# An adaLN transformer block on one core: LayerNorm roots and a memset moved to GpSimd, GpSimd passes tied to VectorE passes, and masked queries built by one copy and eight transfers

## Chip, core and metric

The kernel runs on one core of a Trainium2 chip. The core has TensorE (PE, matrix products into PSUM), VectorE (DVE), ScalarE (ACT), GpSimd (POOL) and SyncE (SP), whose queue issues most of the transfers. The metric is the device time of one execution in microseconds, as the median of several runs. A profile of one execution shows when each instruction ran.

## What is computed

One adaLN block on 2048 tokens of width 512, bf16, with 32 attention heads of width 16 and an MLP of width 1376. The modulation is six rows made from `c`.

```
mod = silu(c) @ w_mod                      # sa, ca, ga, sb, cb, gb
h   = layernorm(x) * (1 + ca) + sa
qkv = h @ wqkv                             # 32 heads, 16 wide
p   = softmax(q k^T / 4)                   # 32 x 2048 x 2048
x   = x + ga * ((p v) @ wo)
h   = layernorm(x) * (1 + cb) + sb
x   = x + gb * (gelu(h @ w1 + b1) @ w2 + b2)
```

## The kernel before, in words

**Tiling.** Queries are taken in four blocks `b` of 512. In a block, heads are taken four at a time: a *quad* is (block, t) with t from 0 to 7, so there are 32 quads. Each quad meets 16 key tiles of 128, four heads each: an *item* is one head's scores of one key tile, 128 x 512. Scores come from row-tiled matmuls (32 of the 128 rows per head, `qk`, L1024). Heads are 16 wide but a row tile is 32, so two heads share a row tile, and the query operand is kept twice, once with the even heads' rows and once with the odd heads' rows, the other rows zero. That is the masked query tile `qm`, 128 x 2 x 512: `q_proj` (L317) makes the projection, `q_evac` (L326) takes it from PSUM in two DVE passes, each multiplied by a column of `qmask`. A new `qm` is made per (block, ch), with ch = t // 2, 16 in all; `used` says when a buffer of the five is free.

**Exponentials on two engines.** ACT takes 12 key tiles of a quad (15 of the first quad), in units of three items (`pA`) and two items (`pB`) by turns (L1076). DVE takes the key tiles 3, 7, 11, 15: it reads one score row from PSUM, adds a bias and writes int16 (a *pass*, L1142); the int16 read as a 16-bit float is an approximate power of two. Three further copies with an offset are made from and to SBUF (*shifts*, L1163), and the four copies are weighed with scaled values `VV` so that the error averages out. PE multiplies all of them with the values (column-tiled, `do_pv`, L1219) into one PSUM bank `od`. DVE copies `od` to SBUF (`o_sb`, L1258); the row of denominators goes through DRAM to a 128 x 16 layout (`d`, `dall`), DVE inverts it (`rp`, L1269), it goes back as a broadcast (`rb`, four transfers), and GpSimd multiplies (`mult`, L1277).

**Order.** All instructions are placed by a planner written in the kernel: it keeps a clock per engine, guesses of durations (`V_PASS`, `EXP`, `TRIP` and others) and labels with the time at which a result is there. `jobs` are rows of (engine, duration, function) with an earliest point `at`, in quads of progress, and `needs`. Each step function (`pe_step`, `dve_step`, `pool_step`, ...) picks the next thing for a free engine. The engines then run their instructions in that order, each held only by semaphores. Where PE would be idle too long, the planner puts in matmuls with zeros (*fill*, L1240). Around the attention lie jobs for the projections, for LayerNorm (`ln_rows`: `ln_var` and `ln_root` are small DVE instructions, an inverse square root by two Newton steps, L221 to L238, and `ln_norm`, L253), for `W_o_pad` (`load_wo`, L404, a memset and eight transfers; `scale_wo`, L410, eight GpSimd passes), and for the output projection and the MLP of each finished block (`tail_jobs`; its last step multiplies on DVE into `tmp`, L689, and adds on GpSimd, L693). `last_tail` does this for the last block after the attention, by hand.

**Start.** Before the planner's part the kernel loads `x`, makes small constants on DVE, warms PE up, normalises block 0, projects its first key and query chunk. The loads of the other blocks are issued behind a DVE memset of one element (L145) that follows the first statistics.

Of the kernel before, what the change touches and what calls it, by code (L numbers as in the profile page):

```python
# [62 lines left out]
KEEP = (5, 18)  # L63

EARLY = 0.95

# [6 lines left out]
FILL_SHARE = 0.75  # L73
V_PASS = 0.61
V_SHIFT = 0.61
V_EVAC = 0.63
# [17 lines left out]
def adaln_block(ctx: ExitStack, tc: tile.TileContext, A_x, A_wqkv, A_wo, B_x, B_w1, B_b1, B_w2, B_b2,  # L94
# [7 lines left out]
    small = ctx.enter_context(tc.tile_pool(name="small", bufs=2))  # L102
    qmp = ctx.enter_context(tc.tile_pool(name="qmp", bufs=5))

# [5 lines left out]
    W_q = res.tile([P, NC, D], BF16, name="W_q")  # L110
    W_o_pad = res.tile([P, 8, D], BF16, name="W_o_pad")
    ga_b = res.tile([P, D], FP32, name="ga_b")
    gb_b = res.tile([P, D], FP32, name="gb_b")
# [63 lines left out]
    magic = const.tile([P, 12], I32, name="magic")  # L177
    nc.vector.memset(magic, 0x5F3759DF)
    zeros = const.tile([P, 32], BF16, name="zeros")
    nc.vector.memset(zeros, 0.0)  # L180
# [8 lines left out]

    ve_ones(VE, 1.0)  # L190

    sc_bf = const.tile([P, NC], BF16, name="sc_bf")
# [50 lines left out]
    def ln_sqrt(st, n):  # L243
        mv = small.tile([P, 12, 2], FP32, name="mv")
        for t in range(n):
            nc.vector.bn_aggr(out=mv[:, t, :], in_=st[:, t, :])
        rs = small.tile([P, 12], FP32, name="rs")
        nc.scalar.activation(out=rs[:, 0:n], in_=mv[:, 0:n, 1], func=ACT.Sqrt, bias=eps_c)
        nc.vector.reciprocal(out=rs[:, 0:n], in_=rs[:, 0:n])
        return mv, rs  # L250

# [67 lines left out]

    def q_evac(ps, ch, b, both=True):  # L320
        t = qmp.tile([P, 2, 512], BF16, name="qm")
        for par in range(2):
            if par and not both:
                nc.scalar.mul(out=t[:, par, :], in_=ps, mul=qmask[:, par:par + 1])
            else:
                nc.vector.tensor_scalar(out=t[:, par, :], in0=ps, scalar1=qmask[:, par:par + 1], scalar2=None,  # L326
                                        op0=ALU.mult)
        qm[(b, ch)] = t

# [73 lines left out]
    def load_wo(j):  # L403
        nc.vector.memset(W_o_pad, 0.0)  # L404
        for r in range(4):
            for par in range(2):
                nc.sync.dma_start(out=W_o4[32 * r:32 * r + 16, :, par, :], in_=wo_v[r][:, :, par, :])
# [46 lines left out]
    def ln_rows(b, src_of, dst_of, key):  # L454

        rows = []

        def var(j):
            st_of[b] = ln_var(st_of[b], 4)

        def root(j):
            st_of[b] = ln_root(*st_of[b])
        rows += [(DVE_, 1.0, var), (DVE_, 1.2, root)]
        for t in range(4):
            def norm(j, t=t):
                mv, rs = st_of[b]
                ln_norm(src_of(), dst_of(), mv, rs, t, t)
            rows.append((DVE_, 0.36, norm))
        return rows
# [21 lines left out]
    def q_job(at, ch, b, needs=()):  # L491
        proj_job(at, lambda ps, js: q_proj(ps, ch, b, js), lambda ps: q_evac(ps, ch, b), [("h", b), *needs],
                 ("q", ch, b), dur=2 * V_EVAC + 0.1)

# [42 lines left out]

    job(4.5, [(DVE_, 2.2, load_wo)], (), "wo_in")
    for t in range(8):
# [20 lines left out]
    def open_late():  # L560
        pro.close()
        lw = ctx.enter_context(tc.tile_pool(name="latew", bufs=1, side="right"))
        W_1 = lw.tile([P, NC, FPAD], BF16, name="W_1")
        nc.gpsimd.memset(W_1[:, :, F:FPAD], 0.0)
        nc.sync.dma_start(out=W_1[:, :, 0:F], in_=B_w1.rearrange("(j p) n -> p j n", p=P))
        W_2 = lw.tile([P, NFC, D], BF16, name="W_2")
        lr = F - (NFC - 1) * P
        nc.gpsimd.memset(W_2[:, NFC - 1, :], 0.0)
        nc.sync.dma_start(out=W_2[:, 0:NFC - 1, :],
                          in_=B_w2[0:(NFC - 1) * P, :].rearrange("(j p) n -> p j n", p=P))  # L570
        nc.sync.dma_start(out=W_2[0:lr, NFC - 1, :], in_=B_w2[(NFC - 1) * P:F, :])
        b1_bf = lw.tile([P, NFC], BF16, name="b1_bf")
        nc.gpsimd.memset(b1_bf, 0.0)
        nc.sync.dma_start(out=b1_bf[:, 0:NFC - 1], in_=B_b1[0:(NFC - 1) * P].rearrange("(j p) -> p j", p=P))
        nc.sync.dma_start(out=b1_bf[0:lr, NFC - 1:NFC],
                          in_=B_b1[(NFC - 1) * P:F].rearrange("(p o) -> p o", o=1))
        b1c = lw.tile([P, NFC], FP32, name="b1c")
        nc.gpsimd.tensor_copy(out=b1c, in_=b1_bf)
        b2r = lw.tile([1, D], BF16, name="b2r")
        nc.sync.dma_start(out=b2r, in_=B_b2.rearrange("(o f) -> o f", o=1))  # L580
        late.update(W_1=W_1, W_2=W_2, b1c=b1c, b2r=b2r)
        tl = ctx.enter_context(tc.tile_pool(name="tailp", bufs=1, side="right"))
        tl2 = ctx.enter_context(tc.tile_pool(name="tailp2", bufs=2, side="right"))
        late.update(tl=tl, tl2=tl2)

    job(6.5, [(SP_, 0.1, lambda j: open_late())],
        ["mod2", "ga", "gb"] + [("k", 3, b) for b in range(NQB)], "late")
    for b in range(NQB - 1):
        for ch in range(NC):

            idx = 4 * (b + 1) + ch - 5
            q_job(8 * b + 2 * ch + 1.3, ch, b + 1, [("used", idx // 4, idx % 4)] if idx >= 0 else [])
# [4 lines left out]
    def tail_jobs(b):  # L597
# [78 lines left out]
        def down(tt):  # L676
# [10 lines left out]
            def mul(j):  # L687
                j.tmp = late["tl2"].tile([P, D], FP32, name="tmp")
                nc.vector.tensor_tensor(out=j.tmp, in0=j.ps, in1=gb_b, op=ALU.mult)  # L689
# [45 lines left out]
    def last_tail():  # L735

        b = NQB - 1
        tl, tl2 = late["tl"], late["tl2"]
        W_1, W_2, b1c = late["W_1"], late["W_2"], late["b1c"]
# [6 lines left out]
        with tc.tile_pool(name="fps", bufs=5, space=PSUM) as fps:  # L746
# [54 lines left out]
            def down_tile(tt, parts=1):  # L801
                o = tl2.tile([P, D], BF16, name="ob")
                tmp = tl2.tile([P, D], FP32, name="tmp")
                n = D // parts
# [143 lines left out]
    nq = len(quads)  # L948
    dall = const.tile([P, nq, 16], FP32, name="dall")
    clock = 0.0  # L950
    free = [0.0, 0.0, 1.0, 0.0, 0.0]
# [188 lines left out]
    def do_pass():  # L1140
        (qi, kt, r), sd, _, last_row, bank = d_items.popleft()
        nc.vector.tensor_scalar(out=t0[(qi, kt)][:, r, :], in0=sd, scalar1=T_BIAS, scalar2=0.0,  # L1142
                                op0=ALU.add, op1=ALU.max)
        end = run(DVE_, V_PASS)
        bank_rel[bank] = end
# [6 lines left out]
    d_prog = [0.0]  # L1152

    def shift_ready():
        if not shifts:
            return False
# [3 lines left out]
    def do_shift():  # L1160
        qi, kt, j = shifts.popleft()
        t16 = tp.tile([P, 4, 512], I16, name="t16")
        nc.vector.tensor_scalar(out=t16, in0=t0[(qi, kt)], scalar1=float(MJ[j]), scalar2=None, op0=ALU.add)  # L1163
        end = run(DVE_, V_SHIFT)
        t16_seq.append((qi, kt, j))
# [154 lines left out]
    def do_job(o, eng):  # L1320
        if o in jobs:
            jobs.remove(o)
            active.append(o)
            if o.hold >= 0:
                o.bank = next(i for i in range(len(banks)) if seen_by(bank_rel[i]))
                bank_rel[o.bank] = INF
        e, dur, fn = o.rows[o.i]
        fn(o)
        if eng == PE_:
# [74 lines left out]
    def dve_step():  # L1404
# [16 lines left out]
        return False  # L1421

    def pool_step():
        o = job_for(POOL_)
        if o is None:
            return False
        do_job(o, POOL_)
        return True
# [63 lines left out]
```

## Time and profile before

| what | us |
|---|---|
| median of 3 runs | 814.64 (811.18 to 816.45) |
| profiled execution, its own time | 815.01 |
| its span, first to last instruction | 813.1 |
| first exponential starts | 14.98 |
| last exponential of the attention ends | 774.7 |
| ACT busy, DVE busy, PE busy, POOL busy | 756.4, 724.8, 770.4, 70.3 |
| granted TensorE clock, mean | 0.995 |

Times within the span count from its first instruction. A line of the costliest groups reads: source line, engine, operation, output and inputs with their shapes, how often, then busy time and mean duration in ns, then the idle time of the engine in front of these instructions and what ended it. A line of the timeline reads: start, duration, engine, line, operation; in brackets the idle time before it and what released it. A matmul's shown duration, 0.38 to 0.39 us for 512 columns, overlaps the next one's; full-rate matmuls start every 0.215 us.

### The profile page before, as it was taken

Reading aid. Unit: us, or ns where it says so; the run is one execution under the profiler, and the core shown is the slowest. Engines: PE = TensorE matmul, PEld = TensorE weight load, DVE = VectorE, ACT = ScalarE, POOL = GpSimd, SP = SyncE. Lnnn points to the kernel's source line nnn. Section 1 sums busy time; section 2 is a strip of 40 time slices with the busy share of each in tenths; the row PEclk is TensorE's granted clock in tenths of the full one; section 3 lists DMA queues with packets and bytes.
Section 4 is the critical chain, followed back from the end, with each engine's and each line's share of the span. In section 5 each row is a group of like instructions: output and inputs, shape, how many; then the busy total and the mean of one; then the engine's idle time right before and its main releaser. Section 6 shows DMA issues by size and latency. Waiting matters only on the chain.

```text
span 813.1 us, 18148 instructions
## 1 busy us (share of the span) xinstructions
PE 770.4 (95%) x7396; PEld 238.1 (29%) x7462; DVE 724.8 (89%) x1306; ACT 756.4 (93%) x681; POOL 70.3 (9%) x62
## 2 busy tenths in 40 slices
PE   7999999988999999999999999999999999999997
PEld 3422222322222222222222322222222222222254
DVE  8879989999998999998998999988998999889663
ACT  5898999998998999999999999999999999999962
POOL 0000000024000000111100000011100000011100
PEclk9999999999899999999999999999999999999999
DMA  9000001023100000000100000010100000010100
GB/s 307 30 1 16 15 16 33 24 70 87 42 15 16 15 16 2 21 16 28 48 16 16 16 13 5 14 29 22 48 15 16 15 3 15 15 28 23 48 2 29
DMA packets 30426, 24.49 MB, mean 30 GB/s; under 512 B 13473, under 2 KB 24194, under 8 KB 30338
## 3 DMA queue, kind: packets, MB, share of 16 engines
q1 hardware_dynamic: 29650, 22.49, 9.7%
q8 instruction: 60, 0.98, 0.5%
q10 hardware_dynamic: 688, 0.79, 0.3%
q14 instruction: 28, 0.23, 0.1%
HBM read 20.65 MB, written 2.61 MB: 29 GB/s over the span
## 4 chain that ended last, share of the span: by engine, by line
PE 48%; ACT 26%; DVE 15%; issue 10%; DMA 1%; POOL 0%; SPq 0%; ACTq 0%; POOLq 0%; DVEq 0%
PE od L1219 15%; ACT pA L1076 14%; ACT pB L1076 9%; PE sA L1024 7%; PE sB L1024 6%; DVE t L1142 5%; DVE t L1163 5%; PE aux L1024 4%; PE od L1240 3%; PE aux L683 3%; PE aux L620 2%; PE aux L303 1%; PE fb L810 1%; PE aux L658 1%; PE aux L332 1%
## 5 line engine op out<-in xcount | busy, mean ns | idle before, releaser
L1076 ACT ACTIVATE pA<-sA 128x1536 bf16<-128x1536 f32 x310 | 469.7, 1515 | 17.0 <-PE sA L1024 7.1
L1142 DVE TENSOR_SCALAR t<-aux 128x512 int16<-128x512 f32 x500 | 327.9, 679 | 31.9 <-PE aux L1024 30.1
L1076 ACT ACTIVATE pB<-sB 128x1024 bf16<-128x1024 f32 x309 | 337.3, 1091 | 6.3 <-PE od L1219 3.6
L1163 DVE TENSOR_SCALAR t<-t 128x2048 int16<-128x2048 int16 x375 | 260.3, 715 | 2.7 <-PE od L1219 1.6
L1024 PE MATMUL aux<-qm,kT 32*128 32x512 bf16 x500 | 178.2, 382 | 6.5 <-DVE t L1142 3.5
L1024 PEld LDWEIGHTS <-kT 32*128 32x128 bf16 x2048 | 76.7, 91 | 267.6 <-issue 262.9
L1219 PE MATMUL od<-pA,VE 128*32 128x512 bf16 x930 | 142.2, 386 | 0.6 <-DVE o_sb L1258 0.5
L1219 PE MATMUL od<-t,VV 128*32 128x512 f16 x1500 | 140.0, 386 | 2.6 <-DVE t L1163 2.4
L1219 PE MATMUL od<-pB,VE 128*32 128x512 bf16 x618 | 141.3, 386 | 0.1
L1024 PE MATMUL sA<-qm,kT 32*128 32x512 bf16 x930 | 124.1, 385 | 10.2 <-ACT pA L1076 5.0
L1024 PE MATMUL sB<-qm,kT 32*128 32x512 bf16 x618 | 121.3, 385 | 5.4 <-ACT pB L1076 2.2
L1277 POOL TENSOR_TENSOR OT<-o_sb,rb 128x512 bf16<-128x512 f32 x31 | 42.2, 1362 | 559.1 <-DMA rb<-d 360.8
L1219 PEld LDWEIGHTS <-VE 128*32 128x32 bf16 x2048 | 50.5, 95 | 95.1 <-issue 82.3
L1240 PE MATMUL od<-hT,zeros 128*32 128x512 bf16 x836 | 75.5, 386 | 0.0
L1219 PEld LDWEIGHTS <-VV 128*32 128x32 bf16 x1500 | 39.8, 95 | 60.6 <-issue 51.7
L1219 PE MATMUL od<-t,VE 128*32 128x512 f16 x500 | 49.4, 386 | 2.7 <-DVE o_sb L1258 2.7
L683 PE MATMUL aux<-W,uG 128*128 128x512 bf16 x120 | 35.5, 383 | 1.6 <-issue 1.6
L658 PE MATMUL aux<-h2T,W 128*128 128x512 bf16 x113 | 35.6, 385 | 0.4 <-issue 0.3
L1240 PEld LDWEIGHTS <-zeros 128*32 128x32 bf16 x864 | 21.8, 95 | 35.9 <-issue 30.8
L663 DVE TENSOR_SCALAR uG<-aux,b1c 128x512 bf16<-128x512 f32 x33 | 24.3, 737 | 4.7 <-PE aux L658 4.7
L620 PE MATMUL aux<-W_o_pad,OT 128*128 128x512 bf16 x88 | 25.6, 382 | 0.7 <-issue 0.5
L693 POOL TENSOR_TENSOR ob<-tmp,xr 128x512 bf16<-128x512 f32 x12 | 15.6, 1304 | 116.5 <-DVE tmp L689 116.5
(157 smaller groups left out, 428.3 us busy)
## 6 DMA issues: line engine op xcount, KB each, us to landing
rb<-d SPq DMA_DIRECT2D x124, 64.0 KB
W_m<-in_w_mod_dram SPq DMA_DIRECT2D x2, 1024.0 KB
xr<-in_A_x_dram SPq DMA_DIRECT2D x4, 512.0 KB
out_dram<-ob SPq DMA_DIRECT2D x15, 128.0 KB
xb<-in_A_x_dram SPq DMA_DIRECT2D x3, 512.0 KB
W<-in_B_w_dram SPq DMA_DIRECT2D x1, 1376.0 KB
W<-in_B_w_dram SPq DMA_DIRECT2D x1, 1280.0 KB
W_m<-in_w_mod_dram SPq DMA_DIRECT2D x1, 512.0 KB
```

The costliest lines, as they stand in the source:

```text
L620: nc.tensor.matmul(out=j.ps, lhsT=OT[(b, t)][:, tt * P:(tt + 1) * P], rhs=W_o_pad[:, t, :], start=False, stop=(t == 7))
L658: nc.tensor.matmul(out=j.ps, lhsT=late["W_1"][:, c, fc * P:(fc + 1) * P], rhs=T["h2"][:, c, :], start=(c == 0), stop=(c == NC - 1))
L663: nc.vector.tensor_scalar(out=T["u"][:, fc, :], in0=j.ps, scalar1=late["b1c"][:, fc:fc + 1], scalar2=None, op0=ALU.add)
L683: nc.tensor.matmul(out=j.ps, lhsT=T["u"][:, fc, tt * P:(tt + 1) * P], rhs=late["W_2"][:, fc, :], start=False, stop=(fc == NFC - 1))
L693: nc.gpsimd.tensor_tensor(out=o, in0=j.tmp, in1=T["x1"][:, tt, :], op=ALU.add)
L1024: nc.tensor.matmul(out=dst, lhsT=kT[32 * r:32 * r + 32, ch, kt * P:(kt + 1) * P], rhs=qm[(b, ch)][32 * r:32 * r + 32, par, :], start=True, ...
L1076: nc.scalar.activation(out=pt[:, 0:n, :], in_=st[:, 0:n, :], func=ACT.Exp, scale=math.log(2.0) / STEP)
L1142: nc.vector.tensor_scalar(out=t0[(qi, kt)][:, r, :], in0=sd, scalar1=T_BIAS, scalar2=0.0, op0=ALU.add, op1=ALU.max)
L1163: nc.vector.tensor_scalar(out=t16, in0=t0[(qi, kt)], scalar1=float(MJ[j]), scalar2=None, op0=ALU.add)
L1219: nc.tensor.matmul(out=od[qi][32 * r:32 * r + 32, :], lhsT=w, rhs=src, start=first, stop=last_)
L1240: nc.tensor.matmul(out=dst[32 * r:32 * r + 32, :], lhsT=zeros, rhs=hT[:, r, 0:512], start=bank is not None, stop=bank is not None)
L1277: nc.gpsimd.tensor_tensor(out=OT[(b, t)], in0=o, in1=j.rb, op=ALU.mult)
```

## The change

- `ln_rows` calls `ln_mean` (DVE, only the aggregation) and `ln_pow` (GpSimd: add EPS, then a power of -0.5 with a constant tile) in place of `ln_var` and `ln_root`. It is used for blocks 1 to 3 at the start and for the three tails; block 0, the last tail and the general path keep what they had.
- A `qm` is no longer made by two masked passes: one DVE pass scales the projection into a staging tile `q_st` (two buffers), and eight transfers on SP of 16 rows each bring the even and odd heads' rows into one of five fixed buffers. Four of these are cleared by GpSimd at the start; the first query chunk still uses the two masked passes, into the fifth buffer. In the planner a query job has a fourth row on SP of 5.5 us.
- `W_o_pad` is cleared by GpSimd, not DVE.
- The planner starts a GpSimd row of over 1 us, once progress is past 0.95, only when DVE starts something that is not a shift, or after a wait of up to 9 us. It puts a one-element GpSimd copy (`mark`) that reads the output of DVE's previous pass or shift in front of it, and keeps shifts from starting until the row's planned end.
- The product `tmp` of the MLP's last step has one buffer, not two.

```
+Q_BUFS = 5
+Q_TRIP = 5.5
+POOL_WAIT = 3.0
+POW = 0.8
...
+    qm_buf = [res.tile([P, 2, 512], BF16, name=f"qm{i}") for i in range(Q_BUFS)]
...
+    for i in range(1, Q_BUFS):
+        nc.gpsimd.memset(qm_buf[i], 0.0)
...
+    def ln_pow(mv, n):
+        rs = small.tile([P, 12], FP32, name="rs")
+        nc.gpsimd.tensor_scalar(out=rs[:, 0:n], in0=mv[:, 0:n, 1], scalar1=EPS, scalar2=None, op0=ALU.add)
+        nc.gpsimd.tensor_tensor(out=rs[:, 0:n], in0=rs[:, 0:n], in1=mhalf[:, 0:n], op=ALU.pow)
+        return mv, rs
...
+    def q_stage(ps):
+        st = qst.tile([P, 512], BF16, name="q_st")
+        nc.vector.tensor_scalar(out=st, in0=ps, scalar1=Q_SCALE, scalar2=None, op0=ALU.mult)
+        return st
+
+    def q_rows(st, ch, b):
+        t = qm[(b, ch)] = qm_buf[(4 * b + ch) % Q_BUFS]
+        for par in range(2):
+            for r in range(4):
+                rows = slice(32 * r + 16 * par, 32 * r + 16 * par + 16)
+                nc.sync.dma_start(out=t[rows, par, :], in_=st[rows, :])
...
-        nc.vector.memset(W_o_pad, 0.0)
+        nc.gpsimd.memset(W_o_pad, 0.0)
...
-        rows += [(DVE_, 1.0, var), (DVE_, 1.2, root)]
+        rows += [(DVE_, 0.6, var), (POOL_, POW, root)]
...
-        proj_job(at, lambda ps, js: q_proj(ps, ch, b, js), lambda ps: q_evac(ps, ch, b), [("h", b), *needs],
-                 ("q", ch, b), dur=2 * V_EVAC + 0.1)
...
+        job(at, [(PE_, 2 * MM, f(0)), (PE_, 2 * MM, f(1)), (DVE_, V_EVAC, stage),
+                 (SP_, Q_TRIP, lambda j: q_rows(j.st, ch, b))], [("h", b), *needs], ("q", ch, b), 2)
...
-    job(4.5, [(DVE_, 2.2, load_wo)], (), "wo_in")
+    job(4.5, [(POOL_, 3.6, load_wo)], (), "wo_in")
...
-                j.tmp = late["tl2"].tile([P, D], FP32, name="tmp")
+                j.tmp = late["tl1"].tile([P, D], FP32, name="tmp")
...
     def shift_ready():
-        if not shifts:
+        if not shifts or clock < port[0]:
             return False
...
+        if eng == POOL_ and dur > 1.0:
+            if dve_now["prev"] is not None and dve_now["start"] > clock - DT / 2:
+                nc.gpsimd.tensor_copy(out=mark[0:1, 0:1], in_=dve_now["prev"][0:1, 0:1])
+            port[0] = clock + dur
...
     def pool_step():
         o = job_for(POOL_)
         if o is None:
             return False
+        if o.rows[o.i][1] > 1.0 and progress() > EARLY and (d_tiles or d_items or shifts):
+            now = dve_now["start"] > clock - DT / 2 and dve_now["free"] and dve_now["prev"] is not None
+            since = pool_since.setdefault((o.label, o.i), clock)
+            if not (now and (d_items or clock > since + POOL_WAIT)) and clock < since + 3.0 * POOL_WAIT:
+                return False
         do_job(o, POOL_)
         return True
```

## Prediction

> **What bounds the kernel now.** I read the page first: the busy shares, then the costliest groups.
>
> ```profile
> span 813.1 us, 18148 instructions
> PE 770.4 (95%) x7396; PEld 238.1 (29%) x7462; DVE 724.8 (89%) x1306; ACT 756.4 (93%) x681; POOL 70.3 (9%) x62
> ...
> PE 48%; ACT 26%; DVE 15%; issue 10%; DMA 1%; POOL 0%; SPq 0%; ACTq 0%; POOLq 0%; DVEq 0%
> ...
> L1076 ACT ACTIVATE pA<-sA 128x1536 bf16<-128x1536 f32 x310 | 469.7, 1515 | 17.0 <-PE sA L1024 7.1
> L1142 DVE TENSOR_SCALAR t<-aux 128x512 int16<-128x512 f32 x500 | 327.9, 679 | 31.9 <-PE aux L1024 30.1
> L1076 ACT ACTIVATE pB<-sB 128x1024 bf16<-128x1024 f32 x309 | 337.3, 1091 | 6.3 <-PE od L1219 3.6
> L1163 DVE TENSOR_SCALAR t<-t 128x2048 int16<-128x2048 int16 x375 | 260.3, 715 | 2.7 <-PE od L1219 1.6
> ...
> L1277 POOL TENSOR_TENSOR OT<-o_sb,rb 128x512 bf16<-128x512 f32 x31 | 42.2, 1362 | 559.1 <-DMA rb<-d 360.8
> ```
>
> Three engines look full, so the shares do not decide. The table by stretch of time does (us; busy time of PE, PEld, DVE, ACT, POOL; clock, DMA).
>
> ```profile
> 150.00:175.00 25.00, 22.47 (x247) 6.98 (x248) 24.64 (x40) 23.26 (x21) 5.13 (x4) 1.00 0.05 13
> 200.00:225.00 25.00, 22.94 (x233) 5.77 (x232) 23.76 (x38) 21.08 (x19) 2.26 (x2) 0.86 0.12 34
> 225.00:275.00 50.00, 47.38 (x463) 14.64 (x464) 45.88 (x89) 45.66 (x41) 2.66 (x2) 1.00 0.06 13
> 275.00:325.00 50.00, 48.30 (x467) 13.88 (x473) 46.44 (x77) 49.95 (x41) 2.54 (x2) 1.00 0.06 13
> 750.00:775.00 25.00, 24.42 (x255) 7.43 (x255) 14.25 (x25) 24.96 (x23) 2.80 (x2) 1.00 0.14 39
> ```
>
> From 275 on ACT is full (49.95 of 50) while DVE has slack, and from 750 to 775 DVE is done early (14.25 of 25). So ACT's exponentials set the length of the attention part. In the trace they follow each other at best every 1.33 us (three items) and 0.90 us (two): 310 x 1.33 + 309 x 0.90 = 690 us of the 760 us between the first (14.98) and the last one's end (774.7). Casts, three Gelus with their table loads take some 27 us; pauses make up the rest. Pauses over 0.15 us in front of the next ACT instruction, start to start, add up to 33 us. Only they, the 15 us before and the 38 us after can change.
>
> The third view is the order of time where ACT pauses longest.
>
> ```profile
> 196.69 4.30 POOL L410 TENSOR_TENSOR W_o_pad<-W_o_pad,ga_b 128x512 bf16<-128x512 bf16 x3
> 196.97 4.56 DVE L1163 TENSOR_SCALAR t<-t 128x2048 int16<-128x2048 int16 x3
> ...
> 200.02 0.40 PE L1219 MATMUL od<-t,VV 128*32 128x512 f16 x4 [0.58 <-DVE t L1163]
> ...
> 201.59 0.62 PE L1219 MATMUL od<-t,VV 128*32 128x512 f16 x4 [0.95 <-DVE t L1163]
> ...
> 202.85 1.45 ACT L1076 ACTIVATE pA<-sA 128x1536 bf16<-128x1536 f32 x1 [2.03 <-PE sA L1024]
> ```
>
> Three shifts (DVE, int16 from and to SBUF) take 4.56 us instead of 3 x 0.68: each that meets a GpSimd pass ends only after it. PE waits for them, then ACT for PE, and matmuls run at 0.60 us instead of 0.39 until about 209 (clock 0.86). Passes from PSUM beside GpSimd stay at 0.67 to 0.69 us. Of 375 shifts, 18 are stretched over 0.72 us, by 13.0 us in all, the longest to 1.76.
>
> **The change, part by part.** The exponentials (619), passes (500) and shifts (375) keep their numbers in the changed program, so ACT's 690 us stay, and a saving on DVE counts only where ACT waits for it.
>
> *GpSimd tied to passes.* The pauses that stand directly behind stretched shifts are 1.4 + 0.3 us near 171, 2.1 + 1.2 + 0.8 + 0.3 near 200 to 208, and 1.0 at 491: 7.1 us. In the changed program, of 51 tied GpSimd operations nearly all follow a shift and have two passes (or copies from PSUM) behind them before the next shift: 2 x 0.60 us start to start. Mark (0.1 to 0.2, from the small GpSimd rows, 0.10 to 0.19) and operation (1.16 to 1.27) take about 1.4, so a shift still waits some 0.2 us, 51 x 0.2 = 10 us, but in small pieces that DVE's slack covers (by the same table it is idle 39 of the 500 us between 225 and 725). If that cover is gone, up to 3 us of it comes back. I take -6.5; bounds -3 and -11 (a quarter of the remaining small pauses, some 17 us, gone too).
>
> *Masked queries.* Removed: 15 of 30 evacuations at 0.74 us (spacing 0.66), 10 us of DVE: hidden, since DVE is not the bound, 0 (bounds -2, 0). Added: 15 x 8 transfers on SP. The eight W_o_pad transfers of before took SP 3.64 us, 0.455 each; from issue to what waits for it a transfer of this queue took 1.7 to 1.8 us (d at 64.16, dall at 65.99). So a query is ready 0.74 + 0.1 + 7 x 0.455 + 1.8 = 5.8 us after its evacuation starts, against 1.4 before: 4.4 later. Where the projection lies a quad or more ahead (twelve jobs for later blocks) that is nothing. For (0,1) it is not: evacuation at 72.33, first use at 76.84, so it would come 72.33 + 5.8 = 78.2, 1.3 late. The order confirms it: between that projection and that first use PE now has 86 matmuls instead of 58, 32 of them fill instead of 16: 28 x 0.054 (four share 0.215 us) = 1.5, with some six more changes of kind at 0.1 (0.32 from a column group to a row in place of 0.215) 2.1. I take +1.8 (bounds 1.3, 2.6). The other two, (0,2) and (0,3), lie 15 and 16 items ahead of use, 6.7 and 7.2 us at 2.23 us for five items: enough. Behind the first of these jobs on SP stands quad 0's denominator; it is issued up to 3.6 us later, but its reciprocal is ten DVE instructions (some 6.5 us) behind, so 0, bound +2 (DVE would wait with passes behind it).
>
> *Rest of the order.* Counting PE's groups between score matmuls in both programs (0.215 a group, 0.1 a change), stretches longer than ACT's pair of 2.23 us, Gelus apart, sum to 1.3 us more in the changed one beyond quad 2; fill grows from 216 to 249 groups. +1.3 (bounds -1, +2.5).
>
> *Root on GpSimd.* Nine small DVE instructions, 15.42 to 17.21: 1.79 us, six times, 10.7 us of DVE. In their place two GpSimd instructions and two hand-overs. The power has no row; the nearest are 0.19 (cast, 128x11) and 1.27 (tensor-tensor, 128x512): with the add and 0.3 of semaphores 0.7 to 1.8, so the chain gets 0 to 1.1 us shorter. Only block 1's first chain is on the path (ACT pauses 2.48 us at 22.7 for its values). Nearest in size is the small row, halved because a power is not a cast: -0.5 (bounds -1.1, +2).
>
> *Memsets on GpSimd.* W_o_pad: DVE loses 1.77; GpSimd needs, from 0.205 (128 columns) and 0.524 (512), 0.83 ns a column, 3.5 us, in which shifts wait; three passes and a copy stand behind it: 0 (bounds -1, +1). Four query buffers at the start, 0.95 us each from about 1.4 us on, beside DVE's first small operations. The row nearest is the 128x4 `var`, 0.91 us instead of 0.17 beside a GpSimd pass. Two operations there are like it (`qmask`, `ce`): two half memsets, +0.9, and all of it is on the path, since the first load of block 1 is issued behind them. Bounds 0 and +3.6 (every small one waits for a whole memset). By the Trainium skill (SBUF — State Buffer, Who interferes with whom) a copy, cast or tensor_scalar in a two-port mode is fully blocked until the GpSimd instruction ends; the 0.91 us agrees, but no run here shows a GpSimd memset doing it. By that rule the one-column operations could be blocked too, and the sum would go towards the upper bound.
>
> Sum against the profiled execution (815.0, its span 813.1 and 1.9 around it; the median of the runs is 814.6): -6.5 + 1.8 + 1.3 - 0.5 + 0.9 = -3.0, **812.0**. The tail's single `tmp` is written and read on DVE in order: nothing.
>
> **Rivals.**
> - *The tie does not hold* (slower). After the mark the multiplication still waits for `rb`; 18 of 31 started when that transfer landed. If it lands over 0.2 us after the mark, the operation runs into the next shift as before, and the -6.5 goes to 0: 818.5. For it: those 18 waits, and SP now carries 55 us more of issues. Against it: six of the 7.1 us stand behind W_o_pad's scaling, which waits for no transfer.
> - *GpSimd is slow at the start* (slower). What block 1's chain gains is replaced by a longer pause of ACT at 22 us. With a power of 3.35 us, the longest elementwise row of the trace (DVE's reciprocal of 128x512), the chain takes 0.19 + 3.35 + 0.3 = 3.8, 2.0 more than now; with that and the memsets' upper bound the time is 812.0 + 0.5 + 2.0 + 2.7 = 817.2. A power over 1.3 us decides it. Against: the first tensor-tensor on GpSimd (74.5) took 1.267 us, like the others. The Trainium skill (GPSIMD Engine Reference, Instruction dispatch) gives about 6 us for the first call of freshly loaded code; no row here shows it, and by it the sum would be near 818 without the memsets.
> - *More pauses go* (faster). If the small pauses were mostly DVE's lateness too, its 22 us of lighter load take 10 of the 17 us: 802. For: DVE is at 24.6 of 25 in 150 to 175. Against: their releaser is PE, and after 275 DVE has 2 to 6 us of slack per 50.
> - *The change does nothing net*: ties gain what the query wait costs, 815.
>
> **How the numbers follow.** Forecast (808 to 816, with the do-nothing case at its edge) 0.55; tie fails 0.17; slow start 0.13; more pauses go 0.15. Two in ten left out at the outside of the outer cases: range 804 to 821. A measurement of this kernel tells about 1% (8.1 us) from no change. Below 806.9: the third rival and a sliver, 0.17. Above 823.2: 0.13 of the 0.30 of the two slower cases, where the upper bounds of the query wait (+0.8), the denominator (+2), the order (+1.2) and DVE's lost cover (+3) come on top. Within: 0.70.
>
> **What would show it.** ACT's exponentials stay at 619, its pauses near 170 and 200 to 208 go, and a pause of about 2 us stands before the third quad's first scores, with PE waiting for `qm<-q_st`. Shifts: mean from 715 ns to about 700, none near 1.7 us. DVE's busy time falls by 20 us or so, without ACT's falling. The first exponential starts about 0.9 us later than 14.98. Wrong would be: shifts of 1.5 us again (tie fails), a power over 1.3 us, the first exponential at 18, or ACT pauses that sum to far less than 28 us.

## The result, and the profile after

The changed kernel took **824.8 us** (median of 4 runs, 823.1 to 828.4) beside 815.6 us (median of 4 runs) of the kernel before: ratio **1.012**, 95% interval 1.008 to 1.016. Predicted were 812.0, range 804 to 821. The profiled execution took 823.1 us with a span of 821.3, 8.2 more than the 813.1 of before.

The page after, its busy shares and ACT's and DVE's largest groups:

```profile
span 821.3 us, 18771 instructions
PE 788.0 (96%) x7594; PEld 240.3 (29%) x7594; DVE 705.7 (86%) x1237; ACT 757.1 (92%) x681; POOL 90.0 (11%) x130
...
L1120 ACT ACTIVATE pA<-sA 128x1536 bf16<-128x1536 f32 x310 | 468.3, 1511 | 12.8 <-PE od L1272 5.4
L1186 DVE TENSOR_SCALAR t<-aux 128x512 int16<-128x512 f32 x500 | 328.4, 681 | 38.1 <-PE aux L1068 36.4
L1120 ACT ACTIVATE pB<-sB 128x1024 bf16<-128x1024 f32 x309 | 335.9, 1087 | 16.0 <-PE od L1272 6.4
L1215 DVE TENSOR_SCALAR t<-t 128x2048 int16<-128x2048 int16 x375 | 259.9, 714 | 6.7 <-PE od L1272 4.7
```

The counts stayed (619 exponentials, 500 passes, 375 shifts), ACT's busy time too (757.1 after 756.4), and DVE lost 19 us. So the extra time is time in which ACT did not compute: its idle time in front of the two groups of exponentials went from 17.0 + 6.3 to 12.8 + 16.0 us.

The table by stretch shows where (after; to be laid beside that of before):

```profile
150.00:175.00 25.00, 24.50 (x251) 6.99 (x248) 22.32 (x40) 23.95 (x22) 2.73 (x4) 1.00 0.09 23
200.00:225.00 25.00, 24.00 (x254) 6.74 (x253) 23.90 (x41) 21.59 (x21) 3.87 (x6) 0.93 0.14 40
225.00:275.00 50.00, 47.67 (x481) 13.82 (x473) 46.47 (x86) 48.39 (x43) 5.12 (x6) 1.00 0.06 16
275.00:325.00 50.00, 48.85 (x452) 13.29 (x444) 45.79 (x75) 48.63 (x40) 2.89 (x4) 1.00 0.08 21
550.00:560.00 10.00, 9.22 (x64) 1.85 (x63) 8.08 (x15) 7.58 (x7) 0.00 (x0) 0.66 0.02 3
750.00:775.00 25.00, 24.69 (x270) 6.98 (x265) 20.96 (x36) 24.85 (x23) 4.00 (x5) 1.00 0.18 50
```

ACT (fourth busy column) gained in the first three rows (23.95 for 23.26, 21.59 for 21.08, 48.39 for 45.66) and lost where it had been full: 48.63 for 49.95 from 275 on, 7.58 for 9.99 between 550 and 560, where the clock column is 0.66. That last stretch in the kernel before:

```profile
550.00:560.00 10.00, 9.84 (x98) 2.85 (x95) 8.65 (x16) 9.99 (x10) 1.16 (x1) 1.00 0.11 29
```

Two sums account for the span of this kernel and of all those below: the start of the first exponential, and ACT's pauses over 0.15 us, counted as in the prediction. Before: 14.98 and 33.0. After: 17.09 and 39.2, so +2.1 and +6.2, against +8.2 of span.

**The start.** The first instructions on GpSimd and DVE (start, duration, engine, line):

```profile
1.35 3.62 POOL L202 MEMSET qm<- 128x1024 bf16 x4
1.44 0.15 DVE L173 TENSOR_SCALAR par_i<-pidx 128x1 int32<-128x1 int32 x1 [1.44 <-POOL pidx L170]
1.63 0.15 DVE L176 CAST pmask<-par_i 128x1 f32<-128x1 int32 x1
1.81 0.15 DVE L177 TENSOR_SCALAR pmask<-pmask 128x1 f32<-128x1 f32 x1
2.00 2.99 DVE L181 TENSOR_SCALAR qmask<-pmask 128x2 f32<-128x2 f32 x1
4.84 0.17 DVE L192 MEMSET ones_row<- 1x128 bf16 x1
```

`qmask` has two columns and takes 0.17 us in the kernel before. Here it ends with the fourth memset, 2.8 us later, and everything behind it on DVE moves: the warm-up's first matmul from 2.67 to 5.37. By the Trainium skill (SBUF — State Buffer, Who interferes with whom) when DVE is in a two-port mode, the engine that issues first holds the shared ports for one whole instruction; the trace agrees that `qmask` is blocked, but it waited for four GpSimd instructions in a row, not for one, and three one-column operations of DVE were not held at all.

**Block 1's LayerNorm.** The root on GpSimd cost what the bounds of the prediction allowed: 1.04 us for the power, a little less than one of GpSimd's 512-column operations (1.15 to 1.27).

```profile
17.13 0.37 DVE L267 BATCH_NORM_AGGREGATE mv<-st 128x2 f32<-128x6 f32 x4
17.59 0.23 POOL L272 TENSOR_SCALAR rs<-mv 128x4 f32<-128x4 f32 x1 [12.61 <-DVE mv L267]
17.90 1.04 POOL L273 TENSOR_TENSOR rs<-rs,mhalf 128x4 f32<-128x4 f32 x1
...
18.98 1.39 DVE L277 TENSOR_SCALAR xb<-xb,mv,rs 128x512 bf16<-128x512 bf16 x4 [1.48 <-POOL rs L273]
```

**The place where ACT had paused longest.** GpSimd's scaling of `W_o_pad` again, with the mark in front of each operation:

```profile
196.09 0.68 DVE L1186 TENSOR_SCALAR t<-aux 128x512 int16<-128x512 f32 x1
196.17 1.15 POOL L443 TENSOR_TENSOR W_o_pad<-W_o_pad,ga_b 128x512 bf16<-128x512 bf16 x1
...
196.69 3.02 DVE L1215 TENSOR_SCALAR t<-t 128x2048 int16<-128x2048 int16 x2
...
197.28 0.18 POOL L1386 COPY mark<-t 1x1 int16<-1x1 int16 x1
197.41 1.15 POOL L443 TENSOR_TENSOR W_o_pad<-W_o_pad,ga_b 128x512 bf16<-128x512 bf16 x1
...
202.77 1.02 ACT L1120 ACTIVATE pB<-sB 128x1024 bf16<-128x1024 f32 x1 [2.71 <-PE aux L1068]
```

GpSimd ran late here, so the mark at 197.28 found its data long there and held nothing. A shift that began at 196.69 waited for the operation in front of it, then for mark and operation behind it: two shifts took 3.02 us in place of 1.28 (back to back without a GpSimd pass), and ACT stopped for 2.9 and 0.8 us. The pauses near 171 are gone (none over 0.15 us is left before the same exponentials), and 0.25 us is left of the 1.0 near 491. Over the kernel 27 shifts are stretched by 12.0 us (18 by 13.0 before).

**New stops.** The longest, apart from the one before the third quad (2.75 us, at 82), stand where PE is never idle. From 429 to 437 (PE's matmuls and ACT's exponentials):

```profile
429.43 0.40 PE L1272 MATMUL od<-pA,VE 128*32 128x512 bf16 x3
429.44 0.39 PE L1272 MATMUL od<-pB,VE 128*32 128x512 bf16 x1
...
431.15 1.04 PE L663 MATMUL aux<-W_o_pad,OT 128*128 128x512 bf16 x4
...
432.62 1.45 ACT L1120 ACTIVATE pA<-sA 128x1536 bf16<-128x1536 f32 x1
432.99 0.39 PE L1068 MATMUL sB<-qm,kT 32*128 32x512 bf16 x2
...
434.82 1.04 PE L663 MATMUL aux<-W_o_pad,OT 128*128 128x512 bf16 x4
435.78 0.39 PE L1272 MATMUL od<-pB,VE 128*32 128x512 bf16 x1
...
436.27 1.02 ACT L1120 ACTIVATE pB<-sB 128x1024 bf16<-128x1024 f32 x1 [2.20 <-PE od L1272]
```

The scores for the next `pB` are there at about 433.4. ACT starts at 436.27, because all four `pB` buffers are taken: PE reads one item of a `pB` at 429.44, and the next, which frees a buffer, only at 435.78, with the output projection (`W_o_pad`) and scores between. That stop is written into the order of PE's instructions.

### The profile page after: what moved, and what is told of

It is laid out like the page before. It is cut to its first block, busy times and chain, and to the rows that moved or that the text cites. A ratio compares the mean times of both kernels' runs of the same rounds, so it can differ in the third digit from the quotient of the medians.

```text
span 821.3 us, 18771 instructions
## 1 busy us (share of the span) xinstructions
PE 788.0 (96%) x7594; PEld 240.3 (29%) x7594; DVE 705.7 (86%) x1237; ACT 757.1 (92%) x681; POOL 90.0 (11%) x130
## 4 chain that ended last, share of the span: by engine, by line
PE 54%; ACT 19%; DVE 15%; issue 7%; DMA 2%; POOL 2%; SPq 0%; POOLq 0%; DVEq 0%; ACTq 0%
PE od L1272 15%; ACT pA L1120 9%; PE sA L1068 7%; PE sB L1068 6%; ACT pB L1120 6%; DVE t L1186 6%; DVE t L1215 5%; PE aux L1068 4%; PE aux L726 3%; PE od L1293 3%; PE aux L663 3%; PE aux L701 3%; ACT uG L715 2%; PE aux L341 1%; PE aux L327 1%
## 5 line engine op out<-in xcount | busy, mean ns | idle before, releaser
L1120 ACT ACTIVATE pA<-sA 128x1536 bf16<-128x1536 f32 x310 | 468.3, 1511 | 12.8 <-PE od L1272 5.4
L1293 PE MATMUL od<-hT,zeros 128*32 128x512 bf16 x940 | 79.8, 383 | 0.0
L1386 POOL COPY mark<-t 1x1 int16<-1x1 int16 x51 | 9.5, 186 | 615.5 <-DVE t L1215 465.9
L1330 POOL TENSOR_TENSOR OT<-o_sb,rb 128x512 bf16<-128x512 f32 x31 | 39.5, 1276 | 14.8 <-DMA rb<-d 10.8
L701 PE MATMUL aux<-h2T,W 128*128 128x512 bf16 x132 | 39.2, 383 | 0.5 <-DVE t L1186 0.4
L726 PE MATMUL aux<-W,uG 128*128 128x512 bf16 x132 | 38.2, 384 | 0.0
L1293 PEld LDWEIGHTS <-zeros 128*32 128x32 bf16 x996 | 23.7, 95 | 37.8 <-issue 30.6
L663 PE MATMUL aux<-W_o_pad,OT 128*128 128x512 bf16 x96 | 27.5, 382 | 0.0
```

Of the source, the lines that this page charges most:

```text
L663: nc.tensor.matmul(out=j.ps, lhsT=OT[(b, t)][:, tt * P:(tt + 1) * P], rhs=W_o_pad[:, t, :], start=False, stop=(t == 7))
L701: nc.tensor.matmul(out=j.ps, lhsT=late["W_1"][:, c, fc * P:(fc + 1) * P], rhs=T["h2"][:, c, :], start=(c == 0), stop=(c == NC - 1))
L726: nc.tensor.matmul(out=j.ps, lhsT=T["u"][:, fc, tt * P:(tt + 1) * P], rhs=late["W_2"][:, fc, :], start=False, stop=(fc == NFC - 1))
L1120: nc.scalar.activation(out=pt[:, 0:n, :], in_=st[:, 0:n, :], func=ACT.Exp, scale=math.log(2.0) / STEP)
L1293: nc.tensor.matmul(out=dst[32 * r:32 * r + 32, :], lhsT=zeros, rhs=hT[:, r, 0:512], start=bank is not None, stop=bank is not None)
L1330: nc.gpsimd.tensor_tensor(out=OT[(b, t)], in0=o, in1=j.rb, op=ALU.mult)
```

## The experiments

After the result there were two theories. **Parts:** the 9 us are the sum of what the changed operations do on the chip (start, query transfers, tie, root). **Order:** the operations cost little, but any change of them or of their planned durations makes the planner write another order of all 18,000 instructions, and the order of before was a favourable one. Every kernel below computes the whole reference. "Planned anew" means that the planner was left to choose; "held" that its inputs stayed as they were and only what a function emits was changed, so that PE's and ACT's orders are identical to those of the kernel named.

| kernel | plan | first exponential | ACT pauses | span | ratio to before |
|---|---|---|---|---|---|
| before | | 14.98 | 33.0 | 813.1 | 1 |
| after | anew | 17.09 | 39.2 | 821.3 | 1.012 (1.008 to 1.016) |
| e1_start | of after | 14.98 | 41.4 | 820.6 | 1.008 (1.005 to 1.010) |
| e2_mask_dve | of after | 17.47 | 48.1 | 831.4 | 1.023 (1.020 to 1.026) |
| e3_no_mark | of after | 17.73 | 41.1 | 823.7 | 1.016 (1.012 to 1.019) |
| e4_q_undone | anew | 16.92 | 31.1 | 813.7 | 0.997 (0.995 to 0.9995) |
| e5_no_tie | anew | 17.01 | 33.1 | 815.6 | 1.006 (1.003 to 1.008) |
| e10_pow_only | anew | 15.45 | 32.8 | 813.9 | 1.007 (1.002 to 1.012) |
| e9_q_early | anew | 16.22 | 40.4 | 820.6 | 1.007 (1.003 to 1.011) |
| e12_q_early_no_tie | anew | 15.42 | 36.7 | 818.6 | 1.004 (1.002 to 1.006) |
| e8_order_b (guess only) | anew | 16.88 | 36.5 | 818.5 | 1.006 (1.002 to 1.009) |
| l4_order_f (guess only) | anew | 17.51 | 36.8 | 819.4 | 1.009 (1.006 to 1.012) |
| e7_order_a (before, guess only) | anew | 15.40 | 39.2 | 820.4 | 1.009 (1.005 to 1.014) |
| l1_order_c (before, guess only) | anew | 15.55 | 39.4 | 820.3 | 1.006 (1.004 to 1.008) |
| l2_order_d (before, guess only) | anew | 16.70 | 34.8 | 816.9 | 1.005 (1.003 to 1.006) |
| f1_pow_held | of before | 15.21 | 35.5 | 815.5 | 1.001 (0.999 to 1.003) |
| f2_q_held | of before | 17.47 | 29.7 | 812.4 | 0.998 (0.996 to 0.9996) |
| f3_both_held | of before | 15.27 | 32.2 | 812.6 | 1.002 (0.999 to 1.005) |

First exponential, pauses and span are of the profiled execution; the two differences add up to that of the span within 1.4 us in every row. The ratio and its interval compare all comparable runs of a kernel with the runs of before made beside them; it is not the quotient of the medians, which for e4 is 0.999, for f3 0.999 and for e9 1.009. In e10 the profiled execution (815.7 us) was the fastest of four with a median of 820.5. In e4, e9, l2 and f2 the first exponential is late for another reason than in the changed kernel: the granted clock there is 0.58 (e4) and 0.72 between 12 and 18 us, and 1.00 in the changed kernel and in f3, which has the same operations at the start as f2.

**The start alone, order of after (e1_start).** The four query buffers are cleared only when block 0's first `hT` is there.

```
-    for i in range(1, Q_BUFS):
-        nc.gpsimd.memset(qm_buf[i], 0.0)
...
+        nc.gpsimd.tensor_copy(out=gate, in_=hT[0:1, 0, 0:1])
+        for i in range(1, Q_BUFS):
+            nc.gpsimd.memset(qm_buf[i], 0.0)
```

> Only the clearing of the four query buffers is moved behind block 0's first hT (a one-element GpSimd copy waits for it); the planned order of everything else is the same. Theory A (the start is held by qmask waiting 2.8 us for all four memsets): the first exponential starts at about 15.0 instead of 17.09, and the time falls by 2.1 us against the changed kernel, to about 822.7. Rival (the start has slack, the memsets only moved a wait): the first exponential stays near 17 and the time near 824.8.

The first exponential is back at 14.98, and the median fell by 3.2 us (821.6), though the two ratios' intervals overlap. So the memsets at the start cost 2 to 3 us, more than the 0.9 predicted and within the bound of 3.6. Two thirds of the loss remain. The profiled spans differ by only 0.7 us: e1's execution was the slowest of its four and has a clock drop more (at 265), the changed kernel's was its fastest.

**The transfers alone, order of after (e2_mask_dve).** The planner still believes in one pass and eight transfers; emitted are two masked DVE passes.

```
-            j.st = q_stage(j.ps)
+            q_evac(j.ps, ch, b)
...
-                 (SP_, Q_TRIP, lambda j: q_rows(j.st, ch, b))], [("h", b), *needs], ("q", ch, b), 2)
+                 (SP_, Q_TRIP, lambda j: None)], [("h", b), *needs], ("q", ch, b), 2)
```

> The planned order is kept instruction by instruction, but each query is masked by two DVE passes into the same buffer, and the 120 transfers are gone (the planner still counts 5.5 us for them). Theory B1 (the stop of ACT before the third quad, 2.7 us, is built into the order by the planner's 5.5 us, with its 33 more fill groups): the stop stays at 1.5 us or more and the time within 1.5 us of the changed kernel. Theory B2 (the transfers are late, eight issues take 5.0 us instead of 3.6): the stop shrinks under 1 us and the time falls by about 2 us. Either way DVE does 15 more passes of 0.66 us.

The stop before the third quad is 2.76 us without a single transfer, 2.75 with them. It is no wait for a transfer; it lies in the order, where the planner, told 5.5 us for a query's way, put the third quad's scores. The time rose by 9 us: 15 more passes of 0.66 us are 9.9 us, so in this fixed order DVE time that the planner had not counted showed nearly in full (time saved on DVE in the order of before did not show, see f3).

**Parts undone, planned anew (e4_q_undone, e5_no_tie, e10_pow_only).** e4: queries as before, the rest as after. e5: no mark, no holding of GpSimd rows or shifts. e10: the kernel before with the root and `W_o_pad`'s memset on GpSimd only (and the fixed `qm` buffers and the single `tmp`).

```
-        job(at, [(PE_, 2 * MM, f(0)), (PE_, 2 * MM, f(1)), (DVE_, V_EVAC, stage),
-                 (SP_, Q_TRIP, lambda j: q_rows(j.st, ch, b))], [("h", b), *needs], ("q", ch, b), 2)
+        proj_job(at, lambda ps, js: q_proj(ps, ch, b, js), lambda ps: q_evac(ps, ch, b), [("h", b), *needs],
+                 ("q", ch, b), dur=2 * V_EVAC + 0.1)
```

```
-                nc.gpsimd.tensor_copy(out=mark[0:1, 0:1], in_=dve_now["prev"][0:1, 0:1])
-            port[0] = clock + dur
+                pass
+            pass
...
-        if o.rows[o.i][1] > 1.0 and progress() > EARLY and (d_tiles or d_items or shifts):
+        if False:
```

> The masked queries are made by two DVE passes again, without transfers and memsets, and planned so; tie, power and W_o_pad's memset stay. Theory A+B: start 2.1 and the stop before the third quad 2.7 go: 4.8 us less than the changed kernel, 820.0, and 4 to 5 more than the kernel before, for the rest. Rival C (the whole loss is the queries): at most 816. Rival D (the loss is order and tie, DVE's 15 passes were worth something): 822 or more.

> No mark, no hold of GpSimd rows, no hold of shifts; queries, power and memsets as changed. Theory E (the tie still brings something, about 3 us, as the pauses near 171 and 491 went): 827 to 829, with shifts stretched by 13 us or more. Rival F (the tie costs more than it brings, through shifts held back and late GpSimd passes): 821 or less.

> The kernel before with the power on GpSimd, W_o_pad's memset on GpSimd and nothing else (queries by two DVE passes, no tie), planned so. If the losses are the queries' (9.8 us with the tie) and the tie's (6.1 us with the queries) each by itself, this is 824.8 - 9.8 - 6.1 = 809, faster than before by 6. If they are one and the same loss seen twice (the tie only hurts a plan with late queries, or the order was unlucky), it is 815 or more.

By the ratios, taken singly, e4 would give the queries 12 us and e5 the tie 5 us of loss, and e10 alone 6 us more than before to the root and the memset: together over 20, where 9 were lost. e4 and e5 each met the expectation that blames its own part (rivals C and F); e10's median of 820.5 met the one by which both were the same loss seen twice. The parts do not add up, which spoke against Parts and led to the next kernels.

**Only a guess changed (e7_order_a, l1_order_c, l2_order_d; e8_order_b, l4_order_f).** The first three are the kernel before, the other two the changed kernel; no operation is changed, only the order and how many fill matmuls the planner adds.

```
-V_PASS = 0.61
+V_PASS = 0.60
```

(e7; l1: `EXP` 0.905 and 1.33 for 0.92 and 1.34; l2: `V_SHIFT` 0.60 for 0.61; e8: `Q_TRIP` 5.7 for 5.5; l4: `POOL_WAIT` 4.0 for 3.0.)

> The kernel before with the planner's guess for a pass at 0.60 us instead of 0.61: the same instructions, in another order. It measures how far the order alone moves the time. Theory L (an order by itself is worth some us either way, and part of the 9 us is that): 3 us or more from 815.5. Rival (order is worth little): within 2 us of it.

> The changed kernel with the planner's guess for a query's transfers at 5.7 us instead of 5.5: the same instructions in another order. Theory L: 3 us or more from 824.8, most likely below it. Rival: within 2 us of it.

> The kernel before, with the planner's guesses for the exponentials set to the measured 0.905 and 1.33 us instead of 0.92 and 1.34: the same instructions in another order. Theory O (the order of the kernel before is a lucky one among many; another costs some 3 to 8 us): 817 to 824, as the 821.2 of e7_order_a. Rival (e7_order_a was the unlucky one): 813 to 816.

> The kernel before with one planner guess changed (a shift 0.60 instead of 0.61), no instruction changed or added but fills; planned anew. Theory Scatter: between 815 and 822, more likely above than below the kernel before, pauses of ACT 34 to 41 us. Rival (the two other orders of before that cost 6 to 7 us were exceptions): within 2 us of before, pauses 31 to 35 us.

> The changed kernel with one planner guess changed (a GpSimd row's longest wait 4.0 times three instead of 3.0 times three), planned anew; the start and all operations as in the changed kernel. Theory Scatter: between 817 and 826, not bound to the changed kernel's 824.8. Rival (the changed kernel's time comes from its operations): 823 to 827.

A change of 0.01 to 0.015 us in a guess costs the kernel before 0.5 to 0.9%, as much as most versions of the changed kernel lost. The clock does not explain it. The time does go with it: the 80 runs of before beside these experiments average 812.7 us where the granted clock is 0.998 or more (16 runs) and 817.6 where it is 0.990 or less (10 runs). But e7, l1 and l2 ran at 0.995 to 0.996 on average, and before at 0.994. One stop that e7 has and before has not (the same kind as at 432 in the changed kernel):

```profile
501.86 1.11 ACT L1076 ACTIVATE pB<-sB 128x1024 bf16<-128x1024 f32 x1
...
502.39 0.39 PE L1024 MATMUL sA<-qm,kT 32*128 32x512 bf16 x3
...
505.39 0.38 PE L1219 MATMUL od<-pA,VE 128*32 128x512 bf16 x1
...
505.87 1.45 ACT L1076 ACTIVATE pA<-sA 128x1536 bf16<-128x1536 f32 x1 [2.89 <-PE od L1219]
```

Scores at 502.4, the exponential at 505.9: again a `pA` buffer that PE read late.

**The operations in the order of before (f1_pow_held, f2_q_held, f3_both_held).** f1: root and `W_o_pad`'s memset on GpSimd. f2: one scaled copy and eight transfers per query, buffers cleared behind block 0's `hT`. f3: both. The planner's rows stay those of before.

```
         def var():
-            st_of[b] = ln_var(st_of[b], 4)
+            st_of[b] = ln_mean(st_of[b], 4)
...
     def q_evac(ps, ch, b, both=True):
...
+        st = qst.tile([P, 512], BF16, name="q_st")
+        nc.vector.tensor_scalar(out=st, in0=ps, scalar1=Q_SCALE, scalar2=None, op0=ALU.mult)
+        for par in range(2):
+            for r in range(4):
+                rows = slice(32 * r + 16 * par, 32 * r + 16 * par + 16)
+                nc.sync.dma_start(out=t[rows, par, :], in_=st[rows, :])
```

> The planned order of the kernel before is held on PE, ACT and DVE; only the inverse roots are made by the power on GpSimd and W_o_pad is cleared there. Theory O (what costs is the new order, not the operations): within 2 us of the kernel before, 812 to 816, or a little faster. Rival (GpSimd's power or its 3.5 us memset stalls shifts and norms): 818 or more, as e10_pow_only's 820.5 in a new order.

> The order of the kernel before is held on PE, ACT and DVE; each query but the first is one scaled copy on DVE and eight transfers on SP (buffers cleared behind the first hT). Theory O: the transfers hold PE once, before the third quad, by 1 to 2.5 us, and DVE has 10 us less to do, so 813 to 818. Rival C (the transfers themselves cost 9 us, through SP's queue or late queries): 822 or more.

> Both of the last two together in the held order, all of the change but the tie. Theory O: the sum of the two, 812 to 818, at least 6 us below the changed kernel's 824.8 although DVE's and GpSimd's operations are the same. Rival: 822 or more.

Root, memset, copies and 120 transfers together cost nothing that can be measured, and save nothing either (f3's interval is -0.1 to +0.5%), though DVE's busy time is 703.9, about that of the changed kernel. From f3, the busy line, and the second query's transfers with the third quad's first scores:

```profile
PE 771.5 (95%) x7396; PEld 237.8 (29%) x7462; DVE 703.9 (87%) x1237; ACT 756.1 (93%) x681; POOL 84.5 (10%) x80
```

```profile
73.71 4.96 SPq L348 DMA_DIRECT2D qm<-q_st  x8
...
77.34 0.39 PE L1048 MATMUL sB<-qm,kT 32*128 32x512 bf16 x2
...
78.17 1.07 ACT L1100 ACTIVATE pB<-sB 128x1024 bf16<-128x1024 f32 x1
```

The exponential at 78.17 holds the third quad's first item; its scores ran at 77.34, while transfers were still being issued until 78.7, and ACT does not pause there. An even quad reads only the half of `qm` that the first four transfers fill. The way of a query that the third quad needs is at most 4.3 us (73.00 to 77.34), not 5.8 as predicted, nor the 5.5 after which the planner lets it go. f2 is 0.2% (0.04 to 0.39%) faster than before; only e4 has a lower ratio.

**Queries earlier, with and without the tie (e9_q_early, e12_q_early_no_tie).** Both clear the buffers late, project block 0's queries earlier and guess 6.8 us for their way; e12 has no tie.

```
-Q_TRIP = 5.5
+Q_TRIP = 6.8
...
-        q_job(1.7 + 2 * (ch - 1) * 0.9, ch, 0)
+        q_job((1.35, 3.1, 5.0)[ch - 1], ch, 0)
```

> The changed kernel with the buffers cleared behind the first hT, the three first query jobs of block 0 asked for a third to half a quad earlier (1.35, 3.1, 5.0 instead of 1.7, 3.5, 5.3), and the planner's trip at the measured 6.8 us instead of 5.5. Theory A+B (start and the stop before the third quad are the queries' whole price): no stop there, 818.5 or less, 3 below e1_start's 821.6. Rival G (the price is spread over all 15 jobs or lies in the order): 821 or more, though the stop is gone.

> The changed kernel without the tie, buffers cleared behind block 0's first hT, block 0's second to fourth query jobs earlier, a longer guess for a query's way through SP; planned anew. Theory Scatter (any new plan of this kernel lands about 4 to 6 us above the order of before, whatever it contains): 817 to 823, ACT pauses of 36 to 41 us. Rival (the queries' stop and the tie are what cost; both are gone): at or below 815, pauses of 33 us or less.

With start and query stop mended (no pause over 0.02 us before the third quad in either) the time is still 0.4 to 0.7% over before, within the scatter of kernels where only a guess differs. Part of that goes with a lower granted clock: 0.983 on average in e9's runs and 0.990 in e12's, beside 0.994 in before; the changed kernel's four have 0.990. e12 without the tie has 24 shifts stretched by 18.9 us, e9 with it 29 by 13.3.

**The mark alone, order of after (e3_no_mark).**

```
-                nc.gpsimd.tensor_copy(out=mark[0:1, 0:1], in_=dve_now["prev"][0:1, 0:1])
+                pass
```

> The changed kernel in its own order, every other instruction in its place; only the 51 small GpSimd copies that hold a tied operation back until the DVE pass has started are left out. Theory T (the tie helps by itself): without it the operations start as soon as their data are there, more shifts are stretched (over 16 us in all instead of 12.0) and the time grows by 2 us or more, to 826 to 830. Rival (the tie moves nothing that ACT waits for; what it changed was the order): within 2 us of the changed kernel, 822.5 to 826.5, stretch between 10 and 15 us. Rival the other way (the mark itself makes operations later and so pushes them into the next shift): under 822, stretch below 10 us.

Its median was 827.7, and 21 shifts are stretched by 15.5 us. At the `W_o_pad` scaling (GpSimd, and DVE's shifts beside it):

```profile
198.77 2.73 DVE L1215 TENSOR_SCALAR t<-t 128x2048 int16<-128x2048 int16 x2
...
199.34 5.86 POOL L443 TENSOR_TENSOR W_o_pad<-W_o_pad,ga_b 128x512 bf16<-128x512 bf16 x4
...
203.21 2.54 DVE L1215 TENSOR_SCALAR t<-t 128x2048 int16<-128x2048 int16 x2
```

Four passes run back to back and catch two pairs of shifts, where with marks one pair was caught; ACT pauses 3.9 us there, with marks 3.7, so what the mark saves lies elsewhere in small pieces. Over the kernel it saves 3.5 us of stretch and 1.9 us of ACT's pauses in one and the same order, and 0.35% of the time by the two ratios, whose intervals overlap. That is 2 to 3 us at most; the two profiles also have their clock drops at different places. The tie's other half, the holding of rows and shifts, is part of the order and stays in e3.

## Why the prediction was wrong, step by step

- **The bound** was right: ACT, with the same 619 exponentials. Start and pauses explain each span, and DVE's 19 us less did not appear in the time.
- **Rest of the order, +1.3 (bounds -1 and +2.5): the step that failed.** Taking from the 6.2 us of added pauses the places seen one by one (where the tie was to help -3.2, query +1.6, root -0.2), 8.0 us are left. The step had been worked out from PE's work between score matmuls, as if an exponential could only be late for its scores. It did not look at when PE reads an earlier `pA` or `pB` and so frees its buffer. The four kernels which share PE's order (after, e1, e2, e3) stop for such a buffer at the same five exponentials for 1.46, 1.22, 2.32, 1.87 (2.28 in e2) and 1.36 us, 8.2 in all, although start, queries and marks differ: these stops belong to the order. At these exponentials the kernel before has 2.1 us, so +6.1. Against that, 4.8 us of stops of the same kind between 240 and 252 in before shrank to 1.5, so -3.3. That is why ACT's whole wait for `od` matmuls, 11.8 us in 9 places, is little more than the 10.4 in 8 of before: not the kind of stop is new, but where and how long PE's order makes ACT wait. The clock drop below adds 3.2, and the last 2 us are pauses under 1 us each.
- **Also in that step, a clock drop.** PE waits 0.78 us until 551.8, then the clock stays halved to about 559 (0.66 over 10 us: 6.8 us at half), matmuls show 0.60 us, and ACT pauses 3.5 us in pieces. e1 has it at the same exponentials as well, e2 too (some 8 us later), e3 not, with the same wait and the same order. So this part can come and go between executions. The drop of before at 200 to 208 did not go either: the clock there is 0.93 over 25 us in the changed kernel, 0.86 before.
- **Tie, -6.5 (bounds -3, -11).** Of the 7.1 us, 3.9 are left around those places, so 3.2 went, at the weak end. That the tie did it is not shown. Before the same exponentials, without any tie and in the order of before, f2 has 3.0 us and f3 2.6 (f1 6.2), with the clock at 1.00 around 200, where in before it was halved from 201.5 on; and e1, with the tie and the changed kernel's order, has 0.2. The pauses there vary by some 4 us between kernels that share an order, which a price read from one profile did not allow for. The first rival's mechanism (mark met early, operation into the next shift) happened, but not through `rb`: GpSimd was behind its plan in the `W_o_pad` scaling, six of the 7.1 us, which the rival's counterargument had taken for safe.
- **Query wait, +1.8.** 2.75 us before the third quad where before had 1.13 one stop later: +1.6. The size was right by luck and the reason wrong: no transfer is waited for, the stop lies in the order (e2), and in the order of before there is none (f2, f3). That the planner's 5.5 us made it fits, but is not shown alone: e7, the kernel before without any transfer, stops 2.0 us at the same exponential. A transfer took SP 0.62 us, not the 0.455 taken from the `W_o_pad` loads.
- **Memsets at the start, +0.9 (bounds 0, +3.6).** 2.1 in the profile, 3.2 by medians: the second term that was too small. The price per blocked operation was wrong: one operation waited for all four memsets, 2.99 us, `ce` for none.
- **Root on GpSimd, -0.5.** Power 1.04 us, within 0.19 to 1.27; from the end of the last aggregate (17.13 + 0.37) to the normalisation at 18.98 are 1.5 us, 0.3 less than the 1.79 of the nine DVE instructions. ACT's pause behind it went from 2.48 to 2.26. Right. The about 6 us that the Trainium skill (GPSIMD Engine Reference, Instruction dispatch) gives for a first call did not show: the first power took 1.04 like the second.
- **More pauses go** (the third rival): ACT's pauses were to come to far less than 33 us; they came to 39.2, and to 32.2 in f3, whose DVE is as light. DVE's lateness was not what they waited for.
- **DVE's savings hidden, 0**, and **W_o_pad's memset, 0**: right, f1 to f3.

So of the 9 us, 2 to 3 are the memsets at the start (e1), and the rest goes with the new order: f3 has all of the change but the tie, with the memsets later, and loses nothing in the order of before.

What stays open: why the order of before is good. Of ten other plans, three of them of the kernel before with no operation changed, nine were 0.4 to 0.9% slower and one (e4) 0.3% faster by its ratio, level by the medians. The three average +0.7%, the seven with changed operations +0.5%; so the operations explain little of the 9 us beyond the start, and the changed kernel's own plan, at 0.8% without its start (e1), is one of the worse ones. That these ten are a fair sample of plans was not tested. Nor was the tie ever run in the order of before, since it changes the order itself.

## What to carry to other kernels

When a planner inside the kernel orders the instructions, a change of operations and a change of order are two changes: hold the order and change only what is emitted, and change only a guess and keep what is emitted, before a part is praised or blamed. For a tuned order, put a scatter of new plans (here 0.4 to 0.9% up in nine of ten) into the prediction as a cost of its own, and look for ACT's lateness in buffers not yet read as well as in scores not yet written. Do not clear large buffers on GpSimd while DVE makes constants that the start waits for.

## What the hardware showed that was not expected

- A blocked DVE instruction can lose again and again to a run of GpSimd instructions: `qmask` 2.99 us behind four memsets; at 196.69 a pair of shifts 3.02 us behind two operations and a mark. One-column DVE operations (0.15 us) passed beside the same memsets.
- Transfers of 16 rows from SBUF to SBUF occupy SP for 0.62 us each (8 in 4.97), the eight loads of `W_o_pad` 0.455 (in before).
- The TensorE clock halved after a wait of PE of only 0.78 us and stayed so for about 6.8 us. The first line below ends that wait; the score matmuls behind it show the drop in their durations:

```profile
551.78 0.40 PE L1272 MATMUL od<-t,VE 128*32 128x512 f16 x4 [0.78 <-DVE o_sb L1311]
552.11 0.61 PE L1068 MATMUL sA<-qm,kT 32*128 32x512 bf16 x3
...
555.99 0.61 PE L1068 MATMUL sA<-qm,kT 32*128 32x512 bf16 x3
...
559.88 0.39 PE L1068 MATMUL sA<-qm,kT 32*128 32x512 bf16 x3
```

The wait alone does not decide it. In e3 PE waits as long at the same place, and the clock stays at 1.00:

```profile
555.61 0.40 PE L1272 MATMUL od<-t,VE 128*32 128x512 f16 x4 [0.78 <-DVE o_sb L1311]
```

The Trainium skill (TensorE: Matmul & The Clock Gate, Part 1) has the clock set by free-running windows of 3.4 us; 6.8 us is two of them, which agrees, though it speaks of an idle window and PE here was busy for most of the time before the drop. In the traces of all these kernels the halved stretches last 3.4, 6.8, 10.2 or 17.1 us, those near the end of the span apart.
